# Identity products at the start of a DeltaNet and PReLU kernel, and its opening dealt anew

## The chip, the cores and the metric

The kernel runs on one core of a Trainium2 chip. Its engines are TensorE (PE in the profile; PEld is its loading of weights), VectorE (DVE), ScalarE (ACT), GpSimd (POOL) and SyncE (SP), whose queue issues nearly all transfers. The metric is the device time in microseconds of one execution, the median of several runs.

## What is computed

First a recurrent attention block, for 4 batches x 8 heads, 768 steps, head size 48; then a feed-forward block over the 3072 tokens (384 wide, 2048 inside):

```
k_n = k / (norm(k) + 1e-06)
for t in range(S):
    y[t]  = q[t] @ state
    v_old = k_n[t] @ state
    state = state + beta[t] * outer(k_n[t], v[t] - v_old)
x = y, turned to (3072, 384)
h = x @ w_in
out = (max(h, 0) + alpha * min(h, 0)) @ w_out
```

All is in f32.

## The kernel before, in words

The sequence is cut into 12 chunks of 64 steps; a chunk for two batches is one step n, so there are 24. Within a chunk the recurrence becomes matrix products with the inverse of a triangular matrix, which is built from the Gram products of the keys. The inverse of the first four steps is found by a small elimination on DVE (`eliminate_small`, L667 on: blocks of 16), that of later steps by `eliminate` (L552 on: blocks of 32). `eliminate` is a generator of pieces: four transposes (`turn_in`, L541), a select and a memset on POOL (L556, L560), and then one round after the other (L566, L572).

The order of the work is written out by hand: each engine runs its instructions in the order in which the program issues them, and waits by semaphores. `part(blocks, n)` gives n pieces of the elimination, `weave` mixes several generators in proportion, and `alongside(products, pieces, ...)` weaves products of the feed-forward block (`ffn_in`, L1076, for chunk 0) with pieces of the conversion of weights.

The opening, for steps 0 to 3: `copy_late` (POOL, L874) copies a key; `squared` (ACT, L387) and `norms` (DVE, L394) give its norm; `key` flips it on TensorE (L431) and gives the copy out of the bank (ACT, L440); `gram` multiplies it with itself (L487); `pick` and `picks` take the 16 x 16 blocks of the Gram product (one on ACT, L642, three on DVE, L644); `raw` takes the rest (ACT, L658); `first_roots` (ACT, L631), `first_reciprocals` (DVE, L635 and L636), `betas` (TensorE, L331; its four signs alternate between DVE, L339, and ACT, L341) and `first_weights` (POOL, L609 to L623) make the weights. `weigh_own` (L653) then starts the small elimination on DVE. Meanwhile TensorE does the products of queries and keys (`queries`, L1564), the flips of keys 5, 6 and 4, those of queries 2 and 3 (`query_flip`), and fillers: `busy(n)` (L1540) issues n products of 512 columns whose result nobody reads. Then follow `first_chunk` (steps 0 and 1) and `second_pair` (steps 2 and 3).

The weights arrive as words that are converted on the chip: `w_in` in 12 pieces of 512 KB, `w_out` in 16. `fetch_in(n)` issues the loads up to piece n on SP, `begin_in(n)` does ACT's part of the pieces up to n (L241, L243), and `conv_in` the rest (DVE, L257; POOL, L264). `pause(n, upto)` writes one element of the space of piece n on POOL and then fetches up to `upto`, so that these loads wait for POOL to come to that place in its order (L1665).

Of the kernel before, what the change touches and what calls it, by code (L numbers as in the profile page):

```python
# [32 lines left out]
C = 64  # L33
HB = 32
W_IN_P = 512
BUSY = 3.5
EARLY = 8
FIRST = 6
LATE = 16
# [1 line left out]
STAGED = 4  # L41
# [3 lines left out]
def kernel(  # L45
# [280 lines left out]
    def betas(first, last, p):  # L326
        n = last - first
        p = p[:, 0 : n * B * H].rearrange("p (c b t h) -> p c b t h", c=n, b=NB, t=2)
        for c in range(n):
            at = (first + c) * 128  # L330
            nc.tensor.transpose(  # L331
                p[:, c].rearrange("p b t h -> p (b t h)"), beta_sb[:, at : at + 128],
                ident[: B * H, : B * H],
            )
        to = beta_t.rearrange("p (c i) b h -> p i c b h", i=2)[:, :, first:last]

        def turned_sign(t, i):
            if i == 0 and first == 0:
                nc.vector.tensor_scalar_mul(to[half(t), i], p[half(i), :, :, t], -1.0)  # L339
            else:  # L340
                nc.scalar.mul(to[half(t), i], p[half(i), :, :, t], -1.0)  # L341

        return [lambda t=t, i=i: turned_sign(t, i) for t in range(2) for i in range(2)]
# [41 lines left out]
    def squared(n):  # L385
        ksq[n] = work.tile([128, H, D], FP32, name="ksq", bufs=2)
        nc.scalar.square(ksq[n], early(n)[:, :, 0:D])  # L387

    def norms(n):
        if n < 4:  # L390
            norm = first_norm[:, n]
        else:
            norm = stats[n] = work.tile([128, H], FP32, name="norm", bufs=EARLY + 3)
        nc.vector.tensor_reduce(out=norm, in_=ksq.pop(n), axis=AXX, op=ALU.add)  # L394
# [72 lines left out]
    def now(pieces):  # L467
        for x in pieces:
            x()
# [159 lines left out]
    def first_roots(c):  # L629
        x = first_norm[:, 2 * c : 2 * c + 2]  # L630
        nc.scalar.sqrt(x, x)  # L631

    def first_reciprocals(c):
        x = first_norm[:, 2 * c : 2 * c + 2]
        nc.vector.tensor_scalar_add(x, x, 1e-6)  # L635
        nc.vector.reciprocal(first_rec[:, 2 * c : 2 * c + 2], x)  # L636

    def pick(n, p, q):

        src, dst = p[:, :, :, q * LB : q * LB + LB], own_part[:, n]  # L640
        if q == 0:
            nc.scalar.mul(dst, src, quarter_of[:, 0:1])  # L642
        else:
            nc.vector.scalar_tensor_tensor(  # L644
                out=dst, in0=src, scalar=quarter_of[:, q : q + 1], in1=dst, op0=ALU.mult, op1=ALU.add
            )

    def picks(n, p):
        for q in range(1, NQ4):
            pick(n, p, q)  # L650
# [894 lines left out]
    def short(n, p):  # L1545

        for _ in range(n):
            nc.tensor.matmul(p[0:32, 0:32], ident[0:32, 0:32], ident[0:32, 0:32])

    def query_flip(n, p):  # L1550

        flip(q_pad[n % NQ], p)
        q_t[n] = beside[steps[n][1]][:, :, :, D : D + C]
        return lambda: nc.scalar.copy(
            q_t[n].rearrange("p t g i -> p g t i")[0:ROWS],
            p.rearrange("p (g t i) -> p g t i", g=G, t=2)[0:ROWS],
        )
# [22 lines left out]
    def first_chunk(convert, mask):  # L1580

        both = (0, 1)
        ahead[0] = 0
        for n in both:
            place_small(n)

        def own(n):
            return own_values(n, ps_big()[:, :, 0:WY])

        def rounds(i):  # L1590
            for x in [one_round(n, i, ps_big()[:, :, 0:WY]) for n in both]:
                now(x)

        now(matrix(0, ps_big()[:, :, 0 : G * C]))
        turn_matrix(0, nc.scalar)
        scale_first(1, nc.vector)
        z_0 = own(0)
        now(z_0)
        turn_values(0, nc.gpsimd)
        convert(1)  # L1600
        now(matrix(1, ps_big()[:, :, 0 : G * C]))
        z_1 = own(1)
        now(z_1)
        turn_values(1, nc.scalar)
        turn_matrix(1, nc.scalar)
        convert(2)
        begin_in(4)
        for n in both:
            mask(n)
        pause(STAGED, STAGED + 2)  # L1610
        for i in range(3):
            rounds(i)
        y_0 = outputs(0, ps_big()[:, :, 0:WY])
        now(y_0)
        convert(2)
        now(outputs(1, ps_big()[:, :, 0:WY]))
        to_ffn(0, ps_ffn())
        to_ffn(1, ps_ffn())
        convert(1)
        for n in range(2, NJ):  # L1620
            place_small(n)
        begin_in()
        ahead[0] = FT * DM
# [39 lines left out]
    def pause(n, upto):  # L1663

        nc.gpsimd.memset(in_stages[n][0:1, 0:1].bitcast(FP32), 0.0)  # L1665
        fetch_in(upto)
# [29 lines left out]
    def key(n):  # L1696
        return flipped(n, ffn_banks[n % 2])

    def gram(n):
        return grams(n, big[n % 3])  # L1700

    for n in (0, 2):
        copy_late(n)
    squared(0)
    copy_0 = key(0)
    norms(0)
    now(copy_0)
    squared(1)
    copy_1 = key(1)
    norms(1)  # L1710
    now(copy_1)
    gram_0 = gram(0)
    signs = betas(0, 1, big[2][:, 0])
    first_roots(0)
    first_reciprocals(0)
    squared(2)
    copy_2 = key(2)
    pick(0, gram_0, 0)
    now(signs)
    picks(0, gram_0)  # L1720
    first_weights(0)
    copy_late(3)
    for n in (6, 5):
        load_early(n)
    fetch_in(1)
    now(copy_2)
    norms(2)
    gram_1 = gram(1)
    squared(3)
    raw(0, gram_0)  # L1730
    copy_3 = key(3)
    copy_late(1)
    load_early(4)
    pick(1, gram_1, 0)
    norms(3)
    first_roots(1)
    now(copy_3)
    gram_2 = gram(2)
    pick(2, gram_2, 0)
    picks(1, gram_1)  # L1740
    first_reciprocals(1)
    first_weights(1)
    for c in range(2):
        first_spread(c, quarter_weight, quarter_of, NQ4)
# [20 lines left out]
        load_v(n)  # L1765
    mask = queries(big[1])
    slopes()
    for n, p in ((5, ffn_banks[0]), (6, big[2][:, 0]), (4, big[2][:, 1])):
        now(flipped(n, p))
    busy(BUSY, big[0][:, 0])  # L1770
    begin_in(2)
    for n in (2, 3):
        query_flip(n, ffn_banks[3 - n])()
    busy(1.5, big[0][:, 0])
    eliminate_small()

    def convert(n):
# [12 lines left out]
    def second_pair():  # L1790

        n, m, x = 2, 3, NJ
        both = (n, m)

        def burst(step, width):
            p = ps_big()
            pieces = []
            for i in range(2):
                pieces += step(n + i, p[:, :, i * width : (i + 1) * width])
            now(pieces)  # L1800

        def keys(k):
            if k == x + 3:
                flip_more(k)
            squared(k)
            norms(k)
            load_early(k + NKE)

        def through(i, p):
            now(through_state(i, None, p))  # L1810

        now(next_state(0))
        scale_first(n)
        pause(STAGED + 2, STAGED + 6)
        scale_first(m)
        alongside(2, 2)
        now(next_state(1))
        keys(x)
        alongside(3, 3)
        burst(matrix, G * C)  # L1820
        for i in both:
            turn_matrix(i, nc.gpsimd)
        now(weigh(x))
        alongside(3, 2)
        for i in both:
            load_q(i + 2)
        fetch_in(12)
        alongside(2, 1)
        keys(x + 1)
        alongside(2, 1)  # L1830
        y = ps_big()
        through(n, y[:, :, 0 : G * D])
        alongside(2, 1)
        through(m, y[:, :, G * D : 2 * G * D])
        now(weigh(x + 1))
        alongside(2, 1)
        now(grams(x))
        alongside(2, 2)
        burst(own_values, G * D)
        pause_out(0, 2)  # L1840
        for i in both:
            turn_values(i, nc.gpsimd)
        alongside(2, 1)
        keys(x + 2)
        fetch_out(3)
        load_v(4)
        alongside(2, 2)
        now(grams(x + 1))
        alongside(2, 2)
        burst(lambda i, p: one_round(i, 0, p), G * D)  # L1850
        now(weigh(x + 2))
        alongside(2, 1)
        keys(x + 3)
        alongside(2, 1)
        now(grams(x + 2))
        alongside(2, 1)
        burst(lambda i, p: one_round(i, 1, p), G * D)
        now(weigh(x + 3))
        alongside(2, 1)
        now(grams(x + 3))  # L1860
        alongside(2, 1)
        burst(lambda i, p: one_round(i, 2, p), G * D)
        fetch_out(4)
        alongside(3, 2, (part(blocks, 4), 4))
        burst(outputs, G * D)
        alongside(4, 3, (part(blocks, 1), 1))
        for i in both:
            to_ffn(i)
        squares(x + 4)
        alongside(2, 1, (part(blocks, 3), 3))  # L1870
        alongside(IN_PARTS - 43, 0, (part(blocks, 1), 1))

    def flip_more(n):
        now(flipped(n, ps_one()))
# [5 lines left out]
            load_v(i + 3)  # L1880
            yield

    blocks, BEGUN, SOON, LAST = eliminate(1), 9, 6, 6
    second_pair()
    weave(
        (part(conv_out, PARTS_OUT - 10 - LAST), PARTS_OUT - 10 - LAST), (ffn_in(1), IN_PARTS - 4),
# [167 lines left out]
```

## Time and profile before

| what | us |
|---|---|
| runs: median (lowest to highest) of 3 | 651.03 (651.0 to 651.74) |
| the profiled execution | 650.03 |
| its span, first to last instruction | 648.2 |
| TensorE busy | 628.7 |
| VectorE busy | 484.5 |
| ScalarE busy | 259.1 |
| GpSimd busy | 126.2 |

The span is shorter than the execution by what lies around it. Most of what TensorE does not do lies in the first 40 us. An f32 product appears as two records of MATMUL and two of LDWEIGHTS. In the order of time a row names its start, its length, engine, line, operation, tiles, the number of instructions merged, and in brackets how long the engine had been idle and what ended that.

### The profile page before, as it was taken

The page shows a single profiled execution, that of the slowest core. Times are in us where ns is not written, and L with a number is a line of the kernel's source. Part 1 is how long each engine was busy: PE and PEld are TensorE (multiplying, and loading weights), DVE is VectorE, ACT ScalarE, POOL GpSimd, SP SyncE. Part 2 cuts the span into 40 slices and gives each one's busy share as a digit, 9 for nine tenths or more (in the row PEclk, how much of TensorE's full clock was granted, in tenths as well). Part 3 has the DMA queues.
Part 4 walks back from the last instruction along what each step waited for, and adds up shares of the span by engine and source line. Part 5 has one row for each costly group of instructions (what it writes and reads, how often), then busy time and mean ns, then how long its engine had stood idle before and what let it go on. Part 6 is the DMA issues. An engine that isn't in the chain of part 4 may idle for free.

```text
span 648.2 us, 21333 instructions
## 1 busy us (share of the span) xinstructions
PE 628.7 (97%) x9147; PEld 555.7 (86%) x9147; DVE 484.5 (75%) x1157; ACT 259.1 (40%) x605; POOL 126.2 (19%) x251
## 2 busy tenths in 40 slices
PE   5799899999999999999999999999999999999997
PEld 4577787566889989989989989989999999999997
DVE  5868889968998787578678578678868568477383
ACT  6667565144644253154144144033045054042240
POOL 7187501010001000000000010000044053062360
PEclk9899999999999999999999999999999999999999
DMA  7859843013511320311211211111221210100000
GB/s 126 197 193 208 219 119 103 16 36 63 99 21 33 75 46 7 69 33 27 55 28 20 42 36 26 38 40 25 42 42 20 52 25 2 38 3 2 25 1 26
DMA packets 106799, 36.89 MB, mean 57 GB/s; under 512 B 99872, under 2 KB 103088, under 8 KB 106704
## 3 DMA queue, kind: packets, MB, share of 16 engines
q1 hardware_dynamic: 104832, 35.03, 24.5%
q8 instruction: 72, 1.18, 0.8%
q10 hardware_dynamic: 1872, 0.49, 0.4%
q14 instruction: 23, 0.19, 0.1%
HBM read 30.78 MB, written 4.72 MB: 55 GB/s over the span
## 4 chain that ended last, share of the span: by engine, by line
PE 83%; DVE 6%; ACT 3%; DMA 3%; POOL 3%; issue 1%; SPq 0%; POOLq 0%; DVEq 0%; ACTq 0%
PE p_ffn L1076 21%; PE p_ffn L1141 17%; PE p_more L1393 8%; PE p_more L1309 5%; PE p_ffn L1119 4%; PE p_ffn L1299 3%; PE p_ffn L1393 3%; PE p_ffn L1304 2%; PE p_pair L431 2%; PE p_pair L808 2%; PE p_pair L748 2%; PE p_pair L918 2%; PE p_pair L931 2%; DMA ke<-in_k_dram 2%; PE p_pair L796 1%
## 5 line engine op out<-in xcount | busy, mean ns | idle before, releaser
L1076 PE MATMUL p_ffn<-xt,w_in 128*128 128x256 f32 x768 | 177.3, 384 | 0.6 <-DVE act L1088 0.5
L1076 PEld LDWEIGHTS p_ffn<-xt,w_in 128*128 128x128 f32 x768 | 142.1, 190 | 20.9 <-issue 1.5
L1086 ACT ACTIVATE act<-p_ffn 128x512 f32<-128x512 f32 x56 | 33.3, 595 | 76.5 <-PE p_ffn L1076 76.3
L1088 DVE SCALAR_TENSOR_TENSOR act<-act,al_t,p_ffn 128x256 f32<-128x256 f32 x112 | 48.5, 474 | 20.5 <-ACT act L1086 20.4
L1333 POOL TENSOR_TENSOR k_t<-k_t 128x128 f32<-128x128 f32 (+1 forms) x48 | 29.5, 614 | 166.9 <-ACT k_t L1328 164.4
L572 DVE TENSOR_TENSOR block<-block,prod 128x30 f32<-128x30 f32 (+9 forms) x150 | 49.8, 332 | 5.2
L420 POOL TENSOR_TENSOR beta_t<-beta_t,rec 128x8 f32<-128x8 f32 x20 | 5.2, 260 | 239.5 <-DVE rec L414 230.0
L566 DVE TENSOR_TENSOR prod<-block 128x30 f32<-128x30 f32 (+9 forms) x150 | 48.9, 326 | 2.8 <-POOL block L556 1.4
L1141 PE MATMUL p_ffn<-w_out,act 128*128 128x192 f32 x288 | 49.6, 328 | 0.0
L974 ACT COPY xt<-p_pair 128x384 f32<-128x384 f32 x22 | 10.5, 479 | 93.2 <-PE p_pair L970 79.4
L1141 PEld LDWEIGHTS p_ffn<-w_out,act 128*128 128x128 f32 x288 | 46.5, 190 | 0.3
L1333 POOL TENSOR_TENSOR block<-block 128x128 f32<-128x128 f32 (+1 forms) x48 | 27.9, 581 | 17.0 <-ACT block L1328 14.5
L1299 PE MATMUL p_ffn<-xt,w_in 128*128 128x256 f32 x96 | 28.7, 381 | 0.5 <-DVE o_sb L1161 0.5
L760 ACT COPY inv<-p_pair 32x256 f32<-32x256 f32 x40 | 14.5, 361 | 24.9 <-DVE u L922 24.1
L1161 DVE TENSOR_TENSOR o_sb<-u,p_ffn 128x192 f32<-128x192 f32 x24 | 7.9, 352 | 20.5 <-PE p_ffn L1141 20.0
L1347 DVE SCALAR_TENSOR_TENSOR act<-block,al_t,act 128x256 f32<-128x256 f32 x32 | 19.2, 642 | 5.3 <-ACT block L1343 5.1
L800 ACT COPY y<-p_pair 128x384 f32<-128x384 f32 x22 | 10.5, 478 | 30.5 <-PE p_pair L796 28.9
L1328 ACT COPY k_t<-p_more 128x512 f32<-128x512 f32 x16 | 9.4, 586 | 31.4 <-PE p_more L1309 26.7
L826 DVE TENSOR_TENSOR r<-v_raw,p_pair 64x192 f32<-64x192 f32 (+1 forms) x60 | 21.1, 352 | 1.0
L1393 PE MATMUL p_more<-w_out,act 128*128 128x192 f32 x128 | 21.9, 329 | 0.0
L922 DVE TENSOR_TENSOR u<-p_pair,wgt 128x384 f32<-128x384 f32 x20 | 11.1, 555 | 14.0 <-PE p_pair L748 14.0
L808 PE MATMUL p_pair<-beside,k_t 48*64 48x112 f32 x704 | 21.4, 259 | 0.2 <-ACT beside L459 0.2
(283 smaller groups left out, 1412.1 us busy)
## 6 DMA issues: line engine op xcount, KB each, us to landing
v_raw<-in_v_dram SPq DMA_DIRECT2D x48, 96.0 KB, 2.9
qp<-in_q_dram SPq DMA_DIRECT2D x48, 96.0 KB, 3.0
out_dram<-o_sb SPq DMA_DIRECT2D x90, 48.0 KB, 1.6
space_out<-in_moe_w_out_dram SPq DMA_DIRECT2D x11, 384.0 KB, 3.7
ke<-in_k_dram SPq DMA_DIRECT2D x43, 96.0 KB, 3.2
kl<-in_k_dram SPq DMA_DIRECT2D x80, 48.0 KB, 2.6
w_out<-in_moe_w_in_dram SPq DMA_DIRECT2D x6, 512.0 KB, 5.4
w_out<-in_moe_w_out_dram SPq DMA_DIRECT2D x5, 384.0 KB, 4.1
```

Of the source, the lines that this page charges most:

```text
L566: nc.vector.tensor_tensor(out=prod, in0=r[:, 0:j, j : j + 1].to_broadcast([128, j, n]), in1=r[:, j : j + 1, j + 1 : HB].to_broadcast([128, ...
L572: nc.vector.tensor_tensor(out=r[:, 0:j, j + 1 : HB], in0=r[:, 0:j, j + 1 : HB], in1=prod, op=ALU.add)
L808: nc.tensor.matmul(p[half(t ^ a), a, g], k_t[n][dims(a), g, half(t)], beside[bp][dims(a), t, g])
L1076: nc.tensor.matmul(p_h[:, i], w_in[:, t, (f + i) * 128 : (f + i + 1) * 128], xt[:, t], start=(t == 0), stop=(t == KT - 1),)
L1086: nc.scalar.activation(g, p_h, ACT.Relu, scale=-1.0)
L1088: nc.vector.scalar_tensor_tensor(out=g[:, i], in0=g[:, i], scalar=al_t[:, f + i : f + i + 1], in1=p_h[:, i], op0=ALU.mult, op1=ALU.add,)
L1119: nc.tensor.matmul(p_o[u], gs[f // 2][:, f % 2, u * 128 : (u + 1) * 128], w_out[:, f], start=(f == 0), stop=(f == FT - 1),)
L1141: nc.tensor.matmul(p, x(i), w(i), start=(i == 0), stop=(i == FP - 1))
L1299: nc.tensor.matmul(p[:, f * 256 : f * 256 + 256], w(2, f), xt[:, 2], start=True, stop=False)
L1309: nc.tensor.matmul(q[:, j], a, b, start=True, stop=True)
L1333: nc.gpsimd.tensor_tensor(out=dst, in0=a, in1=b, op=ALU.add)
L1393: nc.tensor.matmul(p, x(i), w(i), start=(i == 0), stop=(i == FP - 1))
```

## The change

- Nine products of the identity with itself (128 columns, into the first pair of banks, where nobody reads them) are issued ahead of everything else on TensorE.
- The Gram product of key 0 comes before the flip of key 1. The picks of step 0 come before the roots and reciprocals, the signs after the copy of key 1, and the square of key 2 after the signs. Key 3 is copied earlier on POOL.
- The fillers, 3.5 and 1.5 before, are 3.3 before key 4's flip, 2.2 after it, and 1.4 after the query flips. One weight piece is begun before the query flips, the second after them.
- The first pause fetches three weight pieces instead of two, the second two instead of four, and the last of the four goes behind a load of a key.
- Of the pieces of the second elimination in `second_pair` there are 8 (2, 3 and 3) instead of 9 (4, 1, 3 and 1), and 7 instead of 6 after it.

```
-BUSY = 3.5
...
+    def identities(n):
+        for _ in range(n):
+            nc.tensor.matmul(big[0][:, 0, 0:128], ident, ident)
...
-        pause(STAGED, STAGED + 2)
+        pause(STAGED, STAGED + 3)
...
-    for n in (0, 2):
+    identities(9)
+    for n in (0, 2, 3):
         copy_late(n)
     squared(0)
     copy_0 = key(0)
     norms(0)
     now(copy_0)
     squared(1)
+    norms(1)
+    gram_0 = gram(0)
     copy_1 = key(1)
-    norms(1)
+    signs = betas(0, 1, big[2][:, 0])
+    pick(0, gram_0, 0)
+    first_roots(0)
+    picks(0, gram_0)
+    first_reciprocals(0)
     now(copy_1)
-    gram_0 = gram(0)
-    signs = betas(0, 1, big[2][:, 0])
-    first_roots(0)
-    first_reciprocals(0)
+    now(signs)
     squared(2)
     copy_2 = key(2)
-    pick(0, gram_0, 0)
-    now(signs)
-    picks(0, gram_0)
     first_weights(0)
-    copy_late(3)
+    norms(2)
     for n in (6, 5):
         load_early(n)
     fetch_in(1)
     now(copy_2)
-    norms(2)
     gram_1 = gram(1)
     squared(3)
+    norms(3)
     raw(0, gram_0)
     copy_3 = key(3)
     copy_late(1)
     load_early(4)
     pick(1, gram_1, 0)
-    norms(3)
     first_roots(1)
+    picks(1, gram_1)
+    first_reciprocals(1)
     now(copy_3)
     gram_2 = gram(2)
     pick(2, gram_2, 0)
-    picks(1, gram_1)
-    first_reciprocals(1)
     first_weights(1)
...
-    for n, p in ((5, ffn_banks[0]), (6, big[2][:, 0]), (4, big[2][:, 1])):
+    for n, p in ((5, ffn_banks[0]), (6, big[2][:, 0])):
         now(flipped(n, p))
-    busy(BUSY, big[0][:, 0])
-    begin_in(2)
+    busy(3.3, big[0][:, 0])
+    copy_4 = flipped(4, big[2][:, 1])
+    now(copy_4)
+    begin_in(1)
+    busy(2.2, big[0][:, 0])
     for n in (2, 3):
         query_flip(n, ffn_banks[3 - n])()
-    busy(1.5, big[0][:, 0])
+    begin_in(2)
+    busy(1.4, big[0][:, 0])
     eliminate_small()
...
         scale_first(n)
-        pause(STAGED + 2, STAGED + 6)
+        pause(STAGED + 3, STAGED + 5)
         scale_first(m)
         alongside(2, 2)
         now(next_state(1))
         keys(x)
+        fetch_in(STAGED + 6)
...
-        alongside(3, 2, (part(blocks, 4), 4))
+        alongside(3, 2, (part(blocks, 2), 2))
         burst(outputs, G * D)
-        alongside(4, 3, (part(blocks, 1), 1))
+        alongside(4, 3)
         for i in both:
             to_ffn(i)
         squares(x + 4)
         alongside(2, 1, (part(blocks, 3), 3))
-        alongside(IN_PARTS - 43, 0, (part(blocks, 1), 1))
+        alongside(IN_PARTS - 43, 0, (part(blocks, 3), 3))
...
-    blocks, BEGUN, SOON, LAST = eliminate(1), 9, 6, 6
+    blocks, BEGUN, SOON, LAST = eliminate(1), 8, 7, 6
```

## The prediction

> **What bounds the kernel now.** I read the page first (busy shares, then the 40 slices), then the chain that ended last, then tables of engine time cut at the moments when the granted clock changes, then the order in time of each engine up to 97 us, then the landings of the loads.
>
> ```profile
> PE 628.7 (97%) x9147; PEld 555.7 (86%) x9147; DVE 484.5 (75%) x1157; ACT 259.1 (40%) x605; POOL 126.2 (19%) x251
> ...
> PE   5799899999999999999999999999999999999997
> ```
>
> TensorE is the bound, and it is idle mostly in the first slices. The waits confirm it: from 39 us to the end PE waits in few places (under 1.2 us each). So a microsecond taken from the opening or from one of those waits comes off the end. The chain through the opening:
>
> ```profile
> 16.38 5.16 DMA ke<-in_k_dram
> 21.63 0.62 PE p_pair L431 x4
> 22.26 4.71 PE p_pair L1540 x8
> 26.96 0.87 PE p_ffn L431 x8
> 27.84 1.29 PE p_pair L1540 x4
> 29.13 0.67 PE p_pair L858 x32
> ```
>
> PE idles for a key, then runs its fillers (L1540), which delay the first matrix (L858). Columns of the next view: stretch, its length, busy time of PE, PEld, DVE, ACT, POOL, then granted clock, DMA share, GB/s.
>
> ```profile
> 5.31:8.72 3.41, 2.63 (x39) 1.99 (x39) 1.43 (x5) 2.48 (x6) 2.33 (x8) 1.00 1.27 153
> 8.72:12.13 3.41, 3.41 (x56) 2.60 (x59) 2.59 (x8) 2.90 (x11) 2.35 (x8) 1.00 0.71 121
> ...
> 15.55:18.96 3.41, 2.35 (x73) 2.01 (x73) 3.19 (x9) 3.41 (x13) 2.18 (x4) 1.00 0.90 234
> 18.96:22.37 3.41, 0.74 (x5) 0.69 (x6) 3.01 (x12) 1.58 (x5) 0.00 (x0) 1.00 1.13 152
> 22.37:25.78 3.41, 3.41 (x5) 1.35 (x4) 3.03 (x13) 1.74 (x3) 0.00 (x0) 0.50 0.96 288
> ```
>
> After a stretch with 0.74 us of PE work the clock is 0.50 for 3.41 us. The page prints 1.00 before 12 us too, but there four flips take 1.07 to 1.10 us against 0.60 to 0.65 at 17.6 us: that is half speed as well, and full speed came after the fully busy stretch, not after the one with 2.63 of 3.41. In order of time, the places that the change touches:
>
> ```profile
> 7.95 0.51 ACT L387 ACTIVATE ksq<-ke 128x384 f32<-128x384 f32 x1
> ...
> 15.41 0.69 DVE L653 TENSOR_TENSOR same<-same 128x512 f32<-128x512 f32 x1
> ...
> 45.51 0.68 ACT L241 ACTIVATE w_in<-space_out 128x512 uint32<-128x512 uint32 x1 [2.62 <-DMA space_out<-in_moe_w_in_dram]
> ...
> 48.85 0.33 PE L796 MATMUL p_pair<-beside 48*64 48x48 f32 x8 [0.51 <-issue]
> ...
> 51.69 0.68 PE L796 MATMUL p_pair<-beside 48*64 48x48 f32 x32 [0.52 <-ACT y L800]
> ...
> 76.43 1.01 PE L970 MATMUL p_pair<-ident,y 128*128 128x128 f32 x6 [1.13 <-DVE y L937]
> ```
>
> To be seen: ACT squares key 2 at 7.95; the small elimination on DVE starts at 15.41; ACT stands 2.62 us for weight piece 6, and PE loses time twice soon after; PE waits 1.13 us for DVE's y.
>
> **The change part by part** (profiled execution: 650.03 us, span 648.2 and 1.8 around it).
>
> *Identity products.* One f32 product is two records. A filler's half of 512 columns at half clock starts every 0.85 us, so 128 columns take 0.213 and nine products 9 x 2 x 0.213 = 3.84 us; at full clock the nearest row (L1309, 128 columns, four in 0.61 us with a last one of 0.275: 0.112 apart) gives 2.0. I take 3.84. `ident` is ready at 1.47, so they last from 1.55 to 5.4. The first key has landed at 4.30 and its flip ran from 4.39: it is 1.0 us late. If the clock is up by then it takes about 0.6 instead of 1.07, so its copy starts near 6.0 instead of 5.49: 0.5 late. If not, 1.0 late.
>
> *Gram 0 ahead of flip 1.* With the clock up: copy 6.0 to 6.6, Gram 6.65 to 7.34 (0.69 for x32) instead of ending at 8.38; flip 1 to 7.75. What pays is ACT and DVE order. DVE now does the three picks (1.04) before reciprocals and signs: picks from 7.80, reciprocals 8.85 to 9.3, first sign 9.27. The four signs alternate DVE, ACT, DVE, ACT, 0.2 each, the last on ACT at 9.88. The square of key 2, 7.95 before, is now queued on ACT behind them: about 10.0. Copy 2 follows at 10.45 (9.69 before), then the square of key 3, raw and pick 1 (12.1 against 11.34), so the elimination starts at 16.17 instead of 15.41: **0.76 late**. POOL's weights (0.2 to 0.7 late) and the key copy moved ahead of them end no later than DVE. Bounds: no delay (if ACT's squares fitted in as before) and 1.7 (clock still at half: flip and Gram each about 0.45 longer). I take 0.76.
>
> *Fillers.* 3.5 + 1.5 products become 3.3 + 2.2 + 1.4. At full clock one is 0.853, so the first 3.3 take 2.8 us and cover the former idle 18.7 to 21.6; key 4 has landed at 21.54. Then flip, 1.9, query flips 0.9 (queries landed at 23.39), 1.2: PE is done near 26.3, not 29.06. Now DVE ends the wait: own inverse 0 was ready at 27.2, now 27.97. The first matrix starts 1.05 earlier; but behind it DVE still has place 1 and a scaling (to 28.89 + 0.76 = 29.65), so z_0 is copied at 29.65 instead of 30.34, and z_1 at 30.6 against 31.28. ACT's second weight piece (landed 25.98, now behind the query copies) is done by 27.5, before the matrix's copy. The chunk's chain is **0.7 us earlier**. Bounds: -1.4 (no delay of DVE), +0.3 (delay 1.7).
>
> *Pieces 4, 5, 6 at the first pause.* Two issued at 35.87 landed at 39.70 and 40.94, so a third lands near 42.2, less 0.7, instead of 45.42. ACT's 2.62 us is gone. PE's starts were 0.72 us late at 48.1 (its bank waited for ACT's relu at 47.40 and DVE's product behind it) and 0.77 at 50.9 (ACT's y copy): sum 1.5, of which I take **1.35**. Bounds 0 and 1.5. Pieces 7 and 8 keep their pause (POOL after `scale_first`); the key load goes past piece 9 on SP: 9 is issued some 0.4 later, but fewer are outstanding, so it lands before its old 51.83.
>
> *Block turns.* Two transposes (0.6 each) leave DVE's queue ahead of y: y starts near 74.75 instead of 75.81, and PE's wait of 1.13 shrinks by 1.06. They return behind the squares, where DVE then waits for POOL's select and memset (75.96 to 79.69 held them free of charge: 1.27 + 0.3 + 0.1 = 1.65). Queued behind it: three rounds of elimination (1.5) and the activation L1088 of the pair that was at 81.69. It ends at 81.69 + 0.87 - 1.06 + 1.2 + 1.65 - 0.5 (one round fewer) = 83.85; PE needs its bank at 83.96 - 1.06 = 82.9: a wait of 1.0. The next L1088 starts 2.4 us of DVE work later and ends at 87.1 against PE's 83.85 + 2.85 = 86.7: 0.4 more. Net **+0.35**, bounds -1.06 (PE never needs the bank first) and +1.2. Seven later turns instead of six: DVE idles in that stretch, nothing.
>
> Sum: -0.7 - 1.35 + 0.35 = -1.7, so 648.3 for an execution like the profiled one. The timed median, 651.03, stands 1.0 above the profiled run. A half-clock stretch that fell 1 or 2 us earlier, wholly over the fillers, could cost PE that much more, and the change fills that idle time; I credit half: forecast **648.8** in the timed runs.
>
> The Trainium skill (TensorE: Matmul & The Clock Gate, "What's actually happening") says that the gate judges a free-running window of about 3.4 us, which no kernel start resets. The 3.41 us row agrees. By that rule, an estimate, the busy run from 1.55 to 6.45 holds a whole window in only 1.5 of 3.4 phases; the sum would be that of the second case below otherwise.
>
> **The rivals.**
>
> *Cold start.* The nine products do not raise the clock before Gram 0, because no judged stretch is full enough (2.63 of 3.41 did not suffice, 3.41 did; PE stands again from 6.45 for the copy, so the busy run is 4.9 us at half clock). Then DVE starts 1.7 late and the first chunk is 0.3 later, not 0.7 earlier: 648.8 + 1.0 = 649.8.
>
> *The clock falls in the new idle time.* PE now stands from 26.3 to 28.0. A stretch such as 25.8 to 29.2 holds 1.7 of 3.41 us of work; 0.74 let the clock fall, 2.35 did not, so it decides somewhere between. Then the first chunk runs at half clock: a burst of 32 takes 1.13 instead of 0.69, two are on the chain in each of three rounds, one in own values and one in outputs: 8 x 0.44 = 3.5, less where bursts hide behind DVE: 2.8; with the xt flips and the next states 3.7. 651.6 to 652.5: slower than before from 2.3 up. For it: the bursts are never fully busy, so the clock may return late. Against it: at half clock they fill the stretch.
>
> *Piece 6 brings nothing.* If ACT's 2.62 us was not what delayed PE (the first of the two is marked "issue"), or DVE's new wait gives it back: 648.8 + 1.35 = 650.15, to 650.6: within 0.2%.
>
> *All is gained.* Signs cost ACT nothing and y's 1.06 is kept: 648.8 - 0.7 - 1.1 = 647.0.
>
> **How the numbers follow.** About 0.2% (1.3 us) is what a measurement of this kernel can tell from no change: the bounds are 649.7 and 652.3. Forecast 0.46 (own range 647.6 to 650.0; 0.43 faster, 0.03 same). Cold start 0.15 (0.07 faster, 0.08 same). Falling clock 0.20 (0.06 same, 0.14 slower). Piece 6 nothing 0.12, all same. All gained 0.07, faster. Sum 0.57 faster, 0.29 same, 0.14 slower. The range 647.0 to 651.9 leaves out half of the best case and most of the falling clock.
>
> **What would show it.** Right: nine L1551 products from 1.5 to 5.4; four flips in about 0.6 us from 5.4; no half clock at 22 to 26; the first L857 waiting for DVE near 28.0; no long ACT wait for piece 6 and no gaps in L795; the L969 wait under 0.3, but a new wait of about 1 us of L1075 for DVE near 82. Wrong: half clock from 29 on, an elimination that starts after 17, or new PE waits in 40 to 60.

## The result and the profile after

| | before | after |
|---|---|---|
| median of 20 runs, us | 650.76 (648.39 to 652.24) | 653.13 (650.07 to 654.88) |
| ratio, 95% interval | | 1.0034 (1.0023 to 1.0045) |
| span of the profiled execution, us | 648.2 | 651.1 |
| the small elimination starts | 15.41 | 16.66 |
| first matrix of the first chunk | 29.06 | 29.91 |
| first outputs | 35.95 | 38.48 |

The change made the kernel 2.2 us slower (0.34%), and the forecast was 2.2 us faster, with a range that ended at 651.9. The page of after: TensorE's busy row, its granted clock in 40 slices, and a row of the list of DMA queues that the prediction did not read (queue, packets, MB, share):

```profile
PE 634.4 (97%) x9171; PEld 561.2 (86%) x9171; DVE 483.3 (74%) x1157; ACT 258.5 (40%) x605; POOL 126.3 (19%) x251
...
PEclk8799999999999999999999999999999999999999
...
q8 instruction: 72, 1.18, 0.8%
```

TensorE is busy 5.7 us longer, 4.2 of them with the identity products. The table of stretches, cut where the clock may change (columns as in the prediction):

```profile
2.78:6.19 3.41, 3.41 (x18) 3.40 (x17) 1.30 (x6) 1.90 (x3) 2.90 (x16) 1.00 1.13 202
6.19:9.61 3.42, 2.75 (x75) 2.02 (x73) 1.76 (x6) 2.07 (x5) 2.41 (x8) 1.00 0.98 133
9.61:13.02 3.41, 1.45 (x49) 1.00 (x40) 1.47 (x5) 2.89 (x10) 2.40 (x9) 1.00 0.70 128
13.02:16.43 3.41, 2.75 (x41) 2.24 (x41) 3.10 (x11) 2.12 (x9) 1.62 (x7) 0.50 0.69 126
16.43:19.85 3.42, 3.04 (x69) 2.49 (x68) 3.14 (x9) 3.35 (x13) 2.54 (x6) 0.50 1.07 229
19.85:23.26 3.41, 3.41 (x16) 2.60 (x12) 3.00 (x13) 2.51 (x7) 0.00 (x0) 0.50 1.08 153
23.26:26.67 3.41, 3.41 (x13) 1.84 (x12) 3.00 (x14) 0.65 (x2) 0.00 (x0) 1.00 0.94 323
```

The identity products raised the clock at 6.19 us. It fell at 13.02, behind a stretch with 1.45 us of TensorE work (VectorE's and ScalarE's picks and signs hold it up there), and came back at 23.26: behind its first rise, 10.2 us at half speed instead of 3.4. But before that rise the work ran at half speed too, up to 6.19 us here and up to 12.13 in before, so that in sum the two openings hardly differ (16.4 and 15.5 us). In the order of time, what answers to the rows of before:

```profile
10.46 0.52 ACT L386 ACTIVATE ksq<-ke 128x384 f32<-128x384 f32 x1
...
16.66 0.69 DVE L652 TENSOR_TENSOR same<-same 128x512 f32<-128x512 f32 x1
...
34.63 0.72 PE L857 MATMUL p_pair<-act 64*64 64x48 f32 x33 [1.12 <-issue]
...
36.70 0.81 SPq L223 DMA_DIRECT2D w_out<-in_moe_w_in_dram  x2
...
37.55 6.50 SPq L223 DMA_DIRECT2D space_out<-in_moe_w_in_dram  x2
...
38.36 0.25 PE L857 MATMUL p_pair<-r,act 64*64 64x48 f32 x1 [0.74 <-issue]
...
44.59 0.65 ACT L240 ACTIVATE w_in<-space_out 128x512 uint32<-128x512 uint32 x1
...
44.83 0.43 PE L946 MATMUL p_pair<-u,kl 64*64 64x48 f32 x12 [1.40 <-issue]
...
54.25 0.63 PE L795 MATMUL p_pair<-beside 48*64 48x48 f32 x32
...
77.89 1.01 PE L969 MATMUL p_pair<-ident,y 128*128 128x128 f32 x6 [0.69 <-DVE y L936]
...
86.29 2.83 PE L1075 MATMUL p_ffn<-xt,w_in 128*128 128x256 f32 x12 [0.63 <-ACT sums L1085]
...
89.47 2.83 PE L1075 MATMUL p_ffn<-xt,w_in 128*128 128x256 f32 x12 [0.35 <-DVE sums L1087]
```

ScalarE no longer waits for piece 6 (44.59 has no bracket), the wait for y is shorter, and two waits near 86 and 89 us are new: that was forecast. Of the prediction's signs of being wrong one came, a new stop between 40 and 60 us (at 44.83). What was not forecast are three stops of TensorE in the middle of bursts of equal products, marked "issue", which no semaphore explains (1.12, 0.74 and 1.40 us).

How late each point of TensorE's work is against before: +0.85 us at the first matrix, +2.5 at the outputs, +4.0 behind the stop at 44.83, +2.6 at 54.25 (the two gaps in L795 are gone), +1.5 at y, +2.85 at 89.47, +2.9 at the end.

**What the stops are.** Count all of TensorE's records in the trace (MATMUL, LDWEIGHTS and 130 others, mostly semaphores) in order of start. In the kernel before, the stops marked "issue" come ahead of records 961, 1217 and 1729, in after ahead of 961, 1217 and 1473: always 256 apart. The queue list has 72 packets of kind instruction on q8, 1.18 MB, so 16 KB each, and TensorE has 18,424 records before and 18,472 after, 256 to a packet. Each stop ends 1.2 to 1.6 us after such a packet has landed. So TensorE's program arrives in blocks of 256 records, and where it reaches the end of one before the next is usable, it stands. From the traces' packet records (us; "crossed" is the start of the first record of a block, "lag" from there to the start of the next packet, "stop" the start gap at the end of the block):

```
kernel   block     crossed  lag   took  landed   next block starts   stop
before   705-960    30.34   0.58  1.03   31.95   33.48               0.46
before   961-1216   33.48   1.04  1.05   35.57   36.91               0.62
before  1217-1472   36.91   3.44  0.94   41.30   42.80               0.03
before  1473-1728   42.80   3.83  0.94   47.57   48.85               0.73
after    705-960    30.84   1.03  1.36   33.24   34.63               1.33
after    961-1216   34.63   1.15  1.35   37.12   38.35               0.95
after   1217-1472   38.35   4.01  0.88   43.25   44.82               1.61
after   1473-1728   44.82   3.35  0.90   49.08   51.73               0.01
```

The stops sum to 1.8 us before and 3.9 after. The nine identity products are 36 records and the fillers 12 more: 48 records ahead of the first chunk, so that each block ends 48 records earlier in the work. The Trainium skill (Runtime: NRT & Kernel Launch, "Instruction fetch mechanics") says that instructions are refilled in blocks of 16 KiB, 256 of them, ahead of their use, and that crossing a block is mostly hidden. The trace agrees on the size; that it is hidden does not hold here.

### The profile page after: what moved, and what is told of

It is laid out like the page before. It is cut to its first block, busy times and chain, and to the rows that moved or that the text cites. A ratio compares the mean times of both kernels' runs of the same rounds, so it can differ in the third digit from the quotient of the medians.

```text
span 651.1 us, 21381 instructions
## 1 busy us (share of the span) xinstructions
PE 634.4 (97%) x9171; PEld 561.2 (86%) x9171; DVE 483.3 (74%) x1157; ACT 258.5 (40%) x605; POOL 126.3 (19%) x251
## 3 DMA queue, kind: packets, MB, share of 16 engines
q8 instruction: 72, 1.18, 0.8%
## 4 chain that ended last, share of the span: by engine, by line
PE 83%; DVE 7%; ACT 3%; DMA 3%; issue 1%; POOL 1%; SPq 0%; ACTq 0%; POOLq 0%; DVEq 0%
PE p_ffn L1075 21%; PE p_ffn L1140 17%; PE p_more L1392 8%; PE p_more L1308 5%; PE p_ffn L1118 4%; PE p_ffn L1298 3%; PE p_ffn L1392 3%; PE p_ffn L1303 2%; PE p_pair L807 2%; PE p_pair L430 2%; PE p_pair L747 2%; DMA space_out<-in_moe_w_out_dram 2%; PE p_pair L930 2%; PE p_pair L917 2%; PE p_pair L486 1%; PE p_pair L795 1%
## 5 line engine op out<-in xcount | busy, mean ns | idle before, releaser
L954 DVE TENSOR_TENSOR beside<-beside,p_pair 48x384 f32<-48x384 f32 (+1 forms) x38 | 20.8, 547 | 2.4 <-PE p_pair L946 2.2
```

## The experiments

Every kernel was timed in five rounds beside the kernel before, whose medians were 650.28 to 650.86. Differences below are (ratio - 1) x 650.7, with the 95% interval; a time without a sign is a median. The theory after the result: **the number of records ahead of the first chunk decides where the blocks end, and that is most of the loss**. The rivals: the opening's order and clock; the weight pieces; the block turns.

### The number of records alone

Two kernels have the same work in the same order, with the fillers cut into more products (`busy` with a number of parts; 64 columns of `ident` as weights in the second).

```
-    busy(BUSY, big[0][:, 0])               # e1_before_48
+    busy(BUSY, big[0][:, 0], 12)
-    busy(1.5, big[0][:, 0])
+    busy(1.5, big[0][:, 0], 6)
...
-    busy(3.3, big[0][:, 0])                # e2_after_208
+    busy(3.3, big[0][:, 0], 29, 64)
...
+    busy(2.2, big[0][:, 0], 20, 64)
...
+    busy(1.4, big[0][:, 0], 12, 64)
```

> The kernel before, with its fillers cut into 18 products of 128 and 149 columns instead of 6 of up to 512: the same columns, 48 more records on TensorE, as many as the change adds; nothing else is changed. Theory (fetched blocks): the profile lists 72 packets of instructions of 16 KB, one for 256 records of TensorE. In the traces TensorE stops without any wait at records 961, 1217, 1473 and 1729, which are 256 apart, each time until 1.2 to 1.6 us after such a packet has landed: 0.46, 0.62, 0 and 0.73 us in the kernel before (1.8), and 1.33, 0.95, 1.61 and 0 after (3.9). By this, 48 more records move these stops to other products, as the change did, and the kernel before becomes 1.5 to 2.1 us slower: about 652.6, with stops of about 1 us inside bursts between 33 and 45 us. Rival (the number of records does not matter, the stops come from the weight pieces or from the clock): no change, 650.8 within 0.7, and stops as before.

> The changed kernel, with its fillers cut into 61 products of 56 to 59 columns instead of 9 of up to 512: the same columns within 2 in 100, 208 more records, so that with the 48 of the change there are 256 more than before, and the stops fall on the same products as in the kernel before. Theory (fetched blocks): the stops between 30 and 55 us sum to about 1.8 us again instead of 3.9, and the time falls by 1.5 to 2.1 from 653.1, to 651.0 to 651.6, about that of the kernel before. Rival (the number of records does not matter): 653.1 within 0.7, and stops of 0.9 to 1.6 us in the bursts as in the changed kernel.

Measured: with 48 more records the kernel before is 1.4 us slower (0.4 to 2.5), 652.1. Its stops:

```profile
34.01 0.72 PE L858 MATMUL p_pair<-act 64*64 64x48 f32 x33 [0.81 <-issue]
37.73 0.25 PE L858 MATMUL p_pair<-r,act 64*64 64x48 f32 x1 [0.74 <-issue]
43.38 0.43 PE L947 MATMUL p_pair<-u,kl 64*64 64x48 f32 x12 [0.57 <-issue]
```

They stand ahead of the same products as in after (x33, x1 and x12 are left of their bursts), while those of before left x41, x42 and x8. The columns and their order are those of before, and the fillers last as long (4.88 and 1.50 us, 4.87 and 1.46 before), so the number of records moves the stops. The four blocks' stops sum to 2.8 us instead of 1.8. The second kernel's went back to the products of before (its row of L930 leaves x42), and the stops in its blocks from 705 to 1984 sum to 2.2. But 61 small products last longer than 9 wide ones: its first matrix started at 31.69 instead of 29.91, and it was only 0.5 us below after, 652.47 (ratio to before 1.0026, 1.0012 to 1.0040), less than the intervals. The expected 1.5 to 2.1 was missed; the longer fillers would account for it, but that was not tested alone.

A cleaner way back (e5_after_16): the same columns in fewer, wider products.

```
-        for _ in range(n):
-            nc.tensor.matmul(big[0][:, 0, 0:128], ident, ident)
+        for k in (4, 4, n - 8):
+            nc.tensor.matmul(big[0][:, 0, 0 : 128 * k], ident, ident[:, None, :].to_broadcast([128, k, 128]))
...
+    busy(3.0, ...)   busy(2.0, ...)   busy(1.9, ...)
```

> The changed kernel, with the identity products as 3 wide ones (512, 512 and 128 columns) and the fillers as 7 products (3.0, 2.0 and 1.9 instead of 3.3, 2.2 and 1.4): the same columns, and 16 records more than the kernel before instead of 48. Theory (fetched blocks): the stops at the records 256 apart between 30 and 52 us sum to 1.8 to 2.9 us, as in the three traces of kernels with the numbers of the kernel before, instead of 3.9; 0.9 to 1.9 faster than the changed kernel, 651.2 to 652.2. Rival (the number of records does not matter): 653.1 within 0.6.

Measured: 650.97, ratio 1.0012 (0.9996 to 1.0027), 1.4 us below the change (0.2 to 2.6). Its stops sum to 3.0 instead of 3.9, at the upper end of what four traces with the number of records of before have in the blocks from 449 to 1728 (1.8 to 3.1). Five traces with 48 records more have 2.1 to 3.9. So the sum of these stops in one trace does not tell the kernels apart; the times do. Then a larger step, 128 records, on two kernels (e12_before_128 on before, e11_e8_128 on the best kernel, which comes below):

> The kernel before with its fillers cut into 38 products of 64 to 68 columns: 128 records more, the same columns, nothing else. Theory (fetched blocks): with 0, 48 and 128 records more the stops between 28 and 52 us sum to 1.8 to 2.9, 2.8 to 3.9, and now 0.5 to 1.5; the time is about 1 us below the kernel before, 649.8, where 48 records made it 1.4 slower. Rival: 650.8 within 0.7.

> The kernel with pieces and fillers changed (649.1), its 7 fillers cut into 39 products of 88 to 93 columns: 132 records more than before. Theory (fetched blocks): the blocks' ends move 128 records ahead; the first block that lies in the dense part of the first chunk is then crossed while TensorE still has waits for VectorE in it, the stops between 28 and 52 us fall from 2.4 (that kernel's trace: 0.16, 0.53, 0.34 and 1.34) to 0.5 to 1.5, and the time by about 1 us, to 648.2. Rival (no matter how many records): 649.1 within 0.7.

Measured: 655.25 (+4.8 us, 3.4 to 6.2) and 655.93 (+4.9 against before, 3.8 to 6.0; +6.4 against the kernel that it was made from). That the number of records matters is shown; the sign that I expected was wrong. The stops of the four blocks sum to 4.9 and 5.2 us, against 1.8 in before and 2.4 in the best kernel; in both there is one of 2.5 us inside L947, ahead of record 1473, and far behind the first chunk another of 1.3 and 1.2, ahead of record 6081. The first matrix is only 0.6 and 0.9 us later than in the kernels they were made from, so longer fillers are at most that much of the loss. The place of a block's end alone did not tell the size of a stop.

Over all the kernels of this document, whatever else they change, the times go by the records: up to 16 more, 1.6 us below before to 0.8 above; 48 more (five kernels), 1.4 to 3.0 above; 128 to 132 more (three), 4.2 to 4.9 above; and 256 more, a whole block, with its longer fillers, 1.7 above.

### Why a stop is 0 or 2.5 us: the packet waits behind the weight pieces

In the traces so far the packet that is due near 37 to 39 us starts about when the pieces that were issued before it have been moved: at 40.35 in before (two pieces issued at 35.87), 42.37 in after (three at 36.70), 40.77 with 128 records more (two at 36.41), and in the kernel with the block turns alone, where the pieces went out early (34.66), at 39.24, a lag of only 1.14. Three kernels move the pieces: one piece fewer at the first pause of after; the pause of the 128 records' kernel behind two more conversions, so that its pieces are issued at 41.21; and the pause of the best kernel behind one more.

```
-        pause(STAGED, STAGED + 3)          # e13_after_two
+        pause(STAGED, STAGED + 2)
...
-        pause(STAGED + 3, STAGED + 5)
+        pause(STAGED + 2, STAGED + 5)
...
         to_ffn(1, ps_ffn())
         convert(1)
+        pause(STAGED, STAGED + 2)          # e14_128_later: moved here from ahead of the rounds
...
         now(y_0)
         convert(2)
+        pause(STAGED, STAGED + 3)          # e16_e8_later: moved here
```

> The changed kernel with two weight pieces at the first pause and three at the second, instead of three and two. Theory (the instruction packet waits behind the pieces): the packet that started at 42.37 starts one piece (1.35 us) earlier after the crossing (lag 2.7 instead of 4.0), and the stop of 1.6 us in L946 shrinks to about 0.3. In time this is up to 1.3, less what piece 6 costs when it is later (0.75): 652.0 to 653.0. Rival (the lag comes from TensorE's own waits there): lag 4.0 and stop as before, 653.1 to 653.9.

> The kernel before with 128 records more (655.25, with a stop of 2.3 us in L947 at 43.1), in which the first pause stands behind two more conversions on GpSimd, so that its two pieces are issued near 40 instead of 36.4 us, after the request of the packet. Theory (the packet waits behind the pieces): it starts 1.0 to 1.3 us after the crossing instead of 3.8, the stop in L947 is 0 to 0.3, and the time falls by 1.5 to 2.3, to 653.0 to 653.8; the rest of the 4.4 us lies in the stops of 1.28 and 1.06 that lie ahead, and behind. Rival: stop and lag stay, and pieces 4 and 5 come later too: 655.3 to 656.5.

> The kernel with pieces and fillers changed (649.1), with the pause for all three pieces one conversion later on GpSimd (37.6 instead of 36.2 us), about when the packet is requested. Theory: if the packet is in the queue ahead of the pieces, it lags 1.0 to 1.3 and the stop near 43 us goes (0.3 less); if not, it waits for all three, 1.3 us longer than now, and the stop there becomes about 1.7: 650.4. Either is a dose of the same cause; the trace tells which. Rival (pieces do not matter): 649.1, stop and lag as they were.

Measured, lag and stop of the block from 1217: 2.65 and 0.00 (4.01 and 1.61 in after); 1.10 and 0.00 (3.8 and 2.51); 1.23 and 0.00 (4.01 and 0.34). The theory had lag and stop right in all three, but none of the times. The burst with the largest stop, with the pieces at 36.41 us, and then at 41.21:

```profile
36.41 0.81 SPq L224 DMA_DIRECT2D w_out<-in_moe_w_in_dram  x2
...
43.11 0.45 PE L947 MATMUL p_pair<-u,kl 64*64 64x48 f32 x16 [2.29 <-issue]
```

```profile
41.21 0.81 SPq L224 DMA_DIRECT2D w_out<-in_moe_w_in_dram  x2
...
41.42 0.68 PE L947 MATMUL p_pair<-u,kl 64*64 64x48 f32 x32
```

The traffic from 38 to 44 us in 40 slices, after and then the kernel with the pieces at 41.21 (DMA: busy tenths; below, what moved):

```profile
DMA  8959148897998999998999999999893211000000
```

```profile
DMA  0000000300000000000000000009996749565689
GB/s 0 0 0 0 0 0 0 109 0 0 0 0 0 0 0 0 0 0 0 0 0 0 0 0 0 0 0 109 137 137 82 191 191 273 109 164 191 246 328 382
```

In after the engines are full until 42.6, and the packet starts at 42.37. In the other the packet stands alone near 39.1, before any piece. The Trainium skill (DMA: Bandwidth & Descriptors, "Queues, rings and completion order") has each DMA engine take turns between its queues by packets, by which a packet on another queue would wait for one packet of a piece; here it waited for all of 1 to 1.5 MB, and the measurement decides.

In time the cure paid less than the stop: the 128 records' kernel fell from 655.25 to 654.29 (0.7 by the ratios instead of 1.5 to 2.3; the intervals overlap). In its trace pieces 4 and 5 come 4.8 us later, and ahead of 53.24 TensorE waits 2.25 us for an activation of VectorE, which stands behind ScalarE's late pieces. The change with one piece fewer was not faster, 653.72; its trace is of an execution in which the clock stayed at half until 24.7 us, the first matrix started at 30.92, and the clock fell again from 41.75 to 45.17. The best kernel with its pause moved lost its gain, 650.5. A fourth, one piece first and two behind (e15_e8_spread):

> The kernel with pieces and fillers changed (649.1), with one piece at the first pause and a pause more, behind two conversions on GpSimd, that fetches the other two. Theory (the packet waits behind the pieces): the packet near 37 us waits for one piece instead of three, lag 1.2 to 1.6 instead of 4.0, no stop in the products near 43 us (0.34 there), and the next packet is asked for earlier: 0.3 to 1.0 less, 648.1 to 648.8. Rival (pieces 5 and 6 are needed at once): ScalarE waits again for them, and the gain is nothing: 649.1.

Measured: 650.81, 2.2 above the kernel that it was made from, though the lag (1.52) and the stop (0.00) of that block were as expected. In its trace stops of 0.57 and 0.78 came up at other blocks' ends. So that the packet waits for the pieces is shown, but none of the four moves of the pieces was a gain in time beyond its interval.

### The parts of the change

The pieces alone and the block turns alone on the kernel before (the lines of the change's diff, nothing else):

> The kernel before with the change to the weight pieces alone (three at the first pause, two at the second, the last behind a key's load). By the step of the prediction: ScalarE no longer waits 2.62 us for piece 6, and both gaps of TensorE in L796 go: 1.35 us faster, 649.4. Theory now: the first gap (0.73 us, at record 1729) is a stop for fetched instructions and stays or changes with the traffic, the second (0.77) goes: 0.3 to 0.8 faster, 650.0 to 650.5. Rival: three pieces at once delay the instruction packet in flight (1.36 us instead of 1.05 in the changed kernel) and give back all: no change.

> The kernel before with the change to the block turns alone (8 and 7 pieces, 2, 3 and 3 of the eight). By the step of the prediction: y 1.06 us earlier, then two waits of TensorE for VectorE's activations of 1.0 and 0.4: 0.35 us slower. The changed kernel's trace shows y's wait shorter by 0.4 to 0.7 and two waits that sum to 1.4: 0.7 slower, 651.5. Rival: later work takes the difference up, and there is no change.

Measured: the pieces are worth 1.1 us (0.2 to 2.0), 649.78; the turns 0.1 (a gain of 1.0 to a loss of 0.8), 650.53. The pieces' trace:

```profile
45.93 0.67 ACT L241 ACTIVATE w_in<-space_out 128x512 uint32<-128x512 uint32 x1
...
48.84 0.33 PE L796 MATMUL p_pair<-beside 48*64 48x48 f32 x8 [0.85 <-issue]
...
50.98 0.63 PE L796 MATMUL p_pair<-beside 48*64 48x48 f32 x32
```

ScalarE does not wait, and the second gap in L796 is gone (50.98 instead of 51.69). The first is still there, ahead of the same eight products: it was never ScalarE's. The turns' trace:

```profile
74.85 1.01 PE L970 MATMUL p_pair<-ident,y 128*128 128x128 f32 x6 [0.30 <-DVE y L937]
...
83.11 2.83 PE L1076 MATMUL p_ffn<-xt,w_in 128*128 128x256 f32 x12 [0.49 <-DVE act L1088]
...
86.29 2.83 PE L1076 MATMUL p_ffn<-xt,w_in 128*128 128x256 f32 x12 [0.35 <-DVE sums L1088]
```

Against before the flip of y is 0.83 earlier than the work ahead of it (-0.74 to -1.57 us), and the two waits give back 1.24. The same in the change with the old turns (e7_after_old_turns):

> The changed kernel with the block turns of before (9 and 6 pieces, 4, 1, 3 and 1). By the step of the prediction 0.35 us faster than the changed kernel; by the kernel before with the turns alone (y 0.83 earlier, then waits that give back 1.24) 0.4 faster: 652.7. Rival (later work takes it up): 653.1. The trace is to tell, since the difference is smaller than the interval: the waits of 0.6 and 0.35 of L1075 near 86 and 89 us are gone, and the wait for y is above 1 us again.

Measured: 651.86, ratio 1.0023 (1.0010 to 1.0037), 0.7 below the change, which the intervals do not tell from 0.4 or from nothing. In its trace the wait for y is 1.07 again and both waits near 86 and 89 are gone.

The opening: the change with the old order; the new order alone; the change without identities; and identities alone, in three wide products.

> The changed kernel with the opening in the order of before (Gram 0 behind the flip of key 1, ScalarE's square of key 2 ahead of the signs, picks behind the signs); identities, fillers, pieces and turns stay as changed. Theory (the order makes VectorE late and TensorE idle): the small elimination starts at 15.4 to 16.1 instead of 16.6, TensorE is not idle long enough near 10 to 13 us for the clock to fall at 13 us, and the first matrix starts 1 us or more earlier; about 1 us faster than the changed kernel, 652.1. Rival (the opening is hidden: the first chunk is paced by the blocks of instructions): 653.1 within 0.6, with longer stops at records 961 and 1217.

> The kernel before with the changed order of the opening alone; no record more or fewer on TensorE. By the step of the prediction (signs ahead of ScalarE's square of key 2) the elimination starts 0.76 us later where the clock is up and up to 1.7 later where it is not: 16.1 to 17.1 instead of 15.3 to 15.7, and the first chunk follows: 0.5 to 1.2 slower, 651.0 to 651.7. Rival (the fillers end later than VectorE in any case): 650.5 within 0.5.

> The changed kernel without the identity products and with the fillers as 7 products (3.0, 2.0, 1.9): against the one with three wide identity products this takes away the identities alone (12 records fewer). Theory (identities pay: the clock is up from 5 to 7 us on): without them the flips of the keys take 1.1 instead of 0.6 us, the elimination starts at 17.0 to 17.5 instead of 16.7, and the time is 0.3 to 1.0 above that kernel's 651.0 to 651.6. Rival (they only hold up the first key by 1.1 us, since the clock falls again before the queries): the elimination starts at 16.0 to 16.5, and the time is 0.3 to 1.0 below.

> The kernel before with three wide identity products (512, 512, 128 columns) ahead of everything; 12 records more, all else as before. Theory from the differences of earlier runs (the first key's flip is 1.1 us late and the clock, up from 5 to 7 us on, falls again near 13): 0.5 to 1.2 slower, 651.0 to 651.7. Rival (the flips of the keys at full speed make up for the late first key, the elimination starts at 15.0 to 15.4): 650.5 within 0.5.

| kernel | elimination starts | first matrix | ratio to before, 95% |
|---|---|---|---|
| before | 15.41 | 29.06 | |
| after | 16.66 | 29.91 | 1.0034 (1.0023 to 1.0045) |
| after, old order | 15.13 | 28.95 | 1.0022 (1.0002 to 1.0041) |
| before, new order | 16.15 | 29.82 | 1.0003 (0.9989 to 1.0017) |
| after with 16 records | 16.79 | 30.38 | 1.0012 (0.9996 to 1.0027) |
| the same without identities | 16.25 | 30.02 | 0.9999 (0.9988 to 1.0009) |
| before, identities | 15.05 | 29.57 | 1.0009 (0.9996 to 1.0022) |

In the traces the new order starts the elimination later and the identities with the old order start it earlier, as predicted; the first matrix does not follow it closely, since it also waits for the fillers and the clock. In time neither part alone can be told from no change (+0.2, -0.7 to 1.1, and +0.6, -0.3 to 1.4). The change with the old order is 0.8 us below the change, the one without identities 0.8 below the same kernel with them: no more than the intervals. The expected 0.5 to 1.2 for each is not confirmed. The traces missed two expectations as well: with the old order the clock fell all the same (at 12.13), and without identities the elimination started earlier, not later (16.25, as the rival had it).

### A version that beats both

The pieces with the fillers dealt anew, order, turns and opening as before (e8_pieces_fillers), and the same with identities (e10_e8_identities):

> The kernel before with the change to the pieces and with the fillers dealt anew as 7 products (3.0 ahead of key 4's flip, 2.0 behind it, 1.9 behind the query flips; one piece begun ahead of the query flips); 4 records more than before, no identities, order and turns as before. Theory: the pieces alone gave 1.1; fillers in TensorE's idle time before key 4 keep the clock full there, and in the traces in which the last fillers ran at full clock the first matrix started at 27.5 to 27.7 instead of 29.06: 0.5 to 1.2 more, 648.5 to 649.3. Rival (VectorE or the stops set the first chunk anyway): 649.7.

> The kernel with pieces and fillers changed (649.1) and, besides, the three wide identity products ahead of everything; order and turns as before, 16 records more than before. Theory (identities pay where the order is the old one): the elimination starts at 15.0 instead of 15.9, as in the changed kernel with the old order, and the time is up to 0.9 lower, 648.2 to 649.1. Rival (the sum of the parts: what pieces, fillers, turns, order and records leave of the change's 2.2 us is about +1 for the identities): 649.6 to 650.6.

Measured: 649.12, ratio 0.9976 (0.9958 to 0.9993), 1.6 us faster than before and 4.0 below the change by the medians; with identities 649.81, 0.9994 (0.9980 to 1.0008), as the rival had it; the elimination started at 15.57 instead of 15.0. The fillers' own share (0.5 above the pieces alone) is inside the intervals, and its trace does not show the mechanism: there the clock came up at 23.32 only, and the first matrix started at 29.56.

## Why the prediction was wrong

**The step that failed is the sum itself: a term is missing.** The prediction costed the identity products and fillers by their time on TensorE (3.84 us, "one f32 product is two records") and never as records that shift the rest of the program against the blocks of 256. That term is +1.4 us on the kernel before (0.4 to 2.5), and taking 32 of the 48 records out of the change, with its fillers dealt slightly otherwise, gave 1.4 back (0.2 to 2.6). No rival held it either.

**The opening (-0.7) came out at +0.85 in the trace.** The products lasted to 5.74 (5.4 forecast) and the clock rose at 6.19, not before the first flip, which took 0.93 instead of 0.6. ScalarE's square of key 2 started at 10.46 (10.0 forecast) and the elimination 1.25 late instead of 0.76. "Cold start" is real but a matter of the execution: in seven of the eight traces with identities the clock rose between 5.3 and 7.1 us, in one at 24.7. What the prediction did not have is that it does not last: in all seven the clock fell again 6.83 us after its rise, with the old order of the opening too (12.13 and 12.20). This is the rival of the falling clock at another place: in after it fell at 13.02, behind the stretch with 1.45 us, not at 25.8, and TensorE reached the first matrix when its fillers ended.

The prediction also took a matter of the execution for the rule. In ten of the twelve traces without identities the clock first rose at 21 to 26 us, not near 12 as in before, although full stretches of 3.41 us lay ahead of that. The first matrix moves with it: the pieces alone and the turns alone, whose opening is that of before, have it at 27.71 and 27.53 instead of 29.06. So +0.85 between two single traces is no measure of the opening. In time the recorded clock seems to be worth little: of 140 timed executions of the kernel before, the 96 with a recorded mean clock of 0.999 or 1 average 650.6 us, the other 44 650.8. These records begin at the clock's first rise, so they leave out a cold opening. In four traces (e7, e10, e11, e13) the clock also fell inside the first chunk, for 3.4 or 6.8 us between 33.9 and 50.7; in e11 this follows 3.41 us with 1.37 us of work, around the stop of 2.5. What that adds to a stop was not tested.

**Pieces (-1.35): the size was within the interval (-1.1, -2.0 to -0.2), half of its reason was not.** The first of the two gaps was put down to a bank that waited for ScalarE's relu, although its row said "issue". It is the stop ahead of record 1729. It went in the change because the blocks ended elsewhere, and stayed in the kernel with the pieces alone. And the third piece has a price that the step did not have: it holds up the packet by one piece more (lag 4.0 in the change, 3.4 in before).

**Block turns (+0.35): right in the trace.** With the turns alone it has -0.83 and +1.24, so +0.4; the two waits were forecast at 1.0 and 0.4 and measured 0.49 and 0.35, or 0.63 and 0.35 in the change, as the gaps that the profile names; the time alone (-0.1) could not have shown it.

**The credit of 0.5 us for fewer half-clock stretches** is shown by no run: the profiled execution of the change has 10.2 us of them behind the clock's first rise, that of before 3.4.

**What stays open.** The parts done alone sum to about +0.5 us (records +1.4, pieces -1.1, identities +0.6, order +0.2, turns -0.1, fillers -0.5), the change to +2.2. The five measured intervals behind that sum and the change's own, of 0.7 to 1.1 each, make 2.3 in quadrature, so this may be error, or the parts hurt each other, for instance three pieces with blocks that end late. It was not settled. Nor was what sets off a packet: in the dense bursts it lagged the crossing by 0.5 to 1.9 us, but between 18 and 28 us, where TensorE has its fillers and the loads of the opening are moving, by 1.0 to 9.5.

## What to carry to other kernels

Where TensorE stands in the middle of equal products and the profile says "issue", count its records to the stop: if stops are a fixed number apart, the program itself is late, and any added or removed product ahead of a dense part of small products moves them, whatever its own time. Fewer, wider products for the same columns are then worth more than their time, and large loads issued just before a block is due make the stop longer. A difference of 0.2% between two kernels that differ in the number of instructions says little about the idea behind the change, until a kernel with the same idea and another number of instructions has been timed.

## What the runs showed of the hardware that was not expected

- The same work with 48 or 128 more records took 1.4 and 4.8 us longer. Dense blocks of 256 records took at least 2.9 us, mostly 3.2 to 3.9: a packet's lag of mostly 0.6 to 1.2 us, mostly 0.9 to 1.4 for the packet, and 1.2 to 1.7 (once 1.9) until its instructions run.
- A packet of 16 KB waited for up to three pieces of 512 KB on another queue (lag 4.0 us instead of 1.1).
- TensorE's busy share in a stretch of 3.41 us did not tell whether the clock rises. In after 3.04 us of work left it at half; with the turns alone it stayed at half behind two full stretches (7.30 to 14.12; a flip at 19.16 still took 1.10), and with 128 records more it rose behind 2.93. In the execution with identities that stayed cold until 24.7 us a flip at 11.70 still took its half-speed 1.10:

```profile
5.53 1.06 PE L430 MATMUL p_ffn<-ident,ke 128*112 128x128 f32 x4
...
11.70 1.10 PE L430 MATMUL p_ffn<-ident,kl 128*112 128x128 f32 x4
```
